# Five half-row runs for two rows, where there were six runs of 384 columns: the first transform stage of an FNet and long-convolution kernel

## The chip, the cores and the metric

The kernel runs on one core of one Trainium2 chip. The metric is the device time of one execution in microseconds. TensorE (PE) multiplies matrices into PSUM banks, VectorE (DVE) and ScalarE (ACT) do arithmetic and move PSUM to SBUF, GpSimd (POOL) and SyncE (SP) issue transfers, and ACT issues transfers as well. Each engine runs its own instructions in the order in which they stand in the program. An instruction that waits holds up all that stand behind it on its engine.

## The reference

The reference is four layers over a matrix of 2048 rows and 576 columns. Two are Fourier mixing layers, two are gated long convolutions:

```python
    x = x + _A_ref(_layernorm(x, axis=-1), A_dft_seq_re, A_dft_seq_im, A_dft_hid_re, A_dft_hid_im)
    x = x + _B_ref(_layernorm(x, axis=-1), B_k, B_v, B_shift_k, B_ssm_k, B_ssm_D)
    x = x + _A_ref(_layernorm(x, axis=-1), A_dft_seq_re, A_dft_seq_im, A_dft_hid_re, A_dft_hid_im)
    x = x + _B_ref(_layernorm(x, axis=-1), B_k, B_v, B_shift_k, B_ssm_k, B_ssm_D)
```

`_A_ref` takes the real part of a two-dimensional discrete Fourier transform, written as products with cosine and sine matrices (2048 by 2048 along the sequence, 576 by 576 along the columns). `_B_ref` computes `q * (y + kv * ssm_D)`, where `kv` is a convolution of `k` with 4 taps, times `v`, and `y` is the convolution of `kv` with `ssm_k` along the sequence, by a Fourier transform of length 4096. `y` doesn't depend on `x`, so it is computed once, beside the first layer.

## The kernel before

The first Fourier layer is the generator `layer`. It goes through steps `(g, tb, k)`: for each of 4 blocks of output rows, for cosine and for sine, for 16 rows `k` of the input. A step multiplies row `k` with a tile of the sequence matrix (128 by 512) in 14 matmuls of 512 columns: for each of four column blocks `dc` three (high by high, high by low, low by high part, since every float is split into two rounded parts), and two for the 64 columns that remain. They go into the PSUM banks `s` (four) and `rm`. The tile of the sequence matrix comes by a DMA (`load_c`) and is split into its parts by `split`: ACT copies the high part (`mats<-flts`), then DVE subtracts (`mats<-flts,mats`). After 16 steps the four banks are evacuated to `u`.

The convolution's transform is the generator `branch`, and its instructions are put between those of the layer. Its first stage has 16 "rows" `j`, each with two sources of 576 columns: `v` (multiplied by the convolved `k`, which DVE computes in `convolve`: 1152 columns an instruction, `f1f<-f1f`) and `ssm_k`. `f1_split(j, src)` makes the parts of a source: for `v` DVE multiplies first (`f1f<-f1f,flts`), then ACT copies the high part (`f1r<-f1f`, for `ssm_k` `f1r<-flts`) and DVE subtracts (`f1r<-f1f,f1r` and `f1r<-flts,f1r`). From the fifth row on (`j >= K_FIRST`) both sources of a row lie side by side in one tile, 1152 columns. The list `todo` sets the order: `(4, v)`, `(4, ssm_k)`, `(5, v)` and so on, and each entry `n` has two half steps, `2n` and `2n + 1`. The list `visits` says from which half step on a run of columns may be multiplied, and one half step takes at most one.

One run is `f1_products`. It takes two of three PSUM banks `bf` by turns (so that every run shares a bank with the run before it), and multiplies the two halves of the partitions apart: 6 matmuls with 64 rows of weights, three parts by two halves, which leave a bank each. ACT then copies both banks to a buffer (`flts<-bf`) and issues the store to `t_d` (`td<-flts`) from its own queue. In the kernel before, a row from the fifth on has three runs of `VW = 384` columns, from the third half step behind its last split, and a store takes both banks at once; the buffers are three of 768 words (`sp`).

The order on every engine comes from a scheduler, which places the recorded instructions by its own estimates of their durations. Each DMA of SP and ACT tells its landing by one of eight counters, `DMAHW0` to `DMAHW7`, given out by turns; a DMA that is given a counter waits until the one that had it before has landed.

In this text the runs of two rows after the change are called A and B (first row), M (the mixed one), C and D (second row), with the row's number behind the letter. Step `n` is the `n`-th step of the layer, counted over all blocks.

Of the kernel before, what the change touches and what calls it, by code (L numbers as in the profile page):

```python
# [12 lines left out]
AF = mybir.ActivationFunctionType  # L13
# [3 lines left out]
HP = P // 2  # L17
S = 2048
D = 576
J = S // P  # L20
TB = 4
NT = 512
HD = D // 2
# [7 lines left out]
ROWS = (0, 1, 2, 3, 4, 5, 6, 7, 8, 9)  # L31
K_FIRST = 4
F1_16 = 5
VW = 384
F1_END = 42
W_FROM = 41
HOLD = 125
# [16 lines left out]
CRAW = 2  # L54
# [6 lines left out]
SC_AT = 8 + 4 * STAT  # L61
# [5 lines left out]
def fnet_h3_kernel(ctx: ExitStack, tc: tile.TileContext, x, c_mat, w_re, w_im, k_pad, v, shift_k,  # L67
                   ssm_k, ssm_d, f1c, i2c, midc, out):
    nc = tc.nc
# [5 lines left out]
    def mm(ps, lhsT, rhs, first, last, more=False):  # L75
        return nc.tensor.matmul(ps, lhsT, rhs, start=first, stop=last, skip_group_check=more).ins  # L76
# [3 lines left out]
    def turn():  # L80
        given[0] += 1
        return banks[(given[0] - 1) % 3]
# [30 lines left out]
    def flat(words, dt, name):  # L113
        return sb.tile([P, words], dt, tag=name, name=name)
# [29 lines left out]
    def two(v):  # L144
        return v.rearrange("p (a n) -> p a n", a=2)
# [11 lines left out]
    flts = flat(FLT, F32, "flts")  # L157
# [5 lines left out]
    anchor, made, rounded, pows, biased, halved, added, evac, parted, stored = [], [], [], [], [], [], [], [], [], []  # L163
# [39 lines left out]
    t_d = dr.tile([P, 2 * J, 2 * D], F32, name="td")  # L203
# [21 lines left out]
    W = {}  # L225

    def load_w():
        lay(flts, SC_AT + CRAW * NT + 4 * D, ("wl", D, 3))
        wg = region_a(FR, "w").rearrange("p (k n) -> p k n", k=9)
        for ch in (8, *range(8)):  # L230
            w = two(wg[:, ch])
            raw = ring["wl"]()
            if ch < 8:
                asked[:] = [nc.sync.dma_start(raw, (w_re if ch < 4 else w_im)[(ch % 4) * P:(ch % 4 + 1) * P, :]).ins]
            else:
                nc.sync.dma_start(raw[:REM], w_re[NC * P:, :])
                nc.sync.dma_start(raw[REM:], w_im[NC * P:, :])
            for lo, hi, sg in ((0, P, 1 if ch < 4 else -1),) if ch < 8 else ((0, REM, 1), (REM, P, -1)):
                if sg > 0:
                    split(w[lo:hi, 0, :], w[lo:hi, 1, :], raw[lo:hi])  # L240
# [15 lines left out]
    U, seq = {}, []  # L256
# [94 lines left out]
    def branch():  # L351
        f1r = region_b(FR, "f1r")
        lay(f1r, 0, ("xf", 2 * D, 4), ("fc", 2 * P, 5))
        lay(f1r, 0, ("xp", 4 * D, 2))
        at = lay(flts, SC_AT + CRAW * NT, ("so", D, 4), ("land", D, 3))
        lay(flts, SC_AT + CRAW * NT, ("sp", 2 * VW, 3))
        lay(flts, at, ("craw", NT, 1))
        f1f = region_a(F32, "f1f")
        ks = f1f[:, :KR * 2 * D]
# [2 lines left out]
        wt, rows, landed, fcs, paired = [], {}, {}, {}, []  # L362
# [23 lines left out]
        def convolve():  # L386
            for i in range(J // 2):
                if not wt:
                    load_w4()
                load_k(i + KR - 1)  # L390
                rp = rows[i] = two(ring["rp"]())
                for t in range(4):
                    out_t = two(tmp) if t else rp
                    for n, k in k_rows(2 * i + t):
                        nc.vector.tensor_tensor(out_t[:, n], k, wt[3 - t][:, n], OP.mult)  # L395
                    yield
                    if t == 1:
                        load_k(i + KR)
                    if t:
                        nc.vector.tensor_tensor(rp, rp, out_t, OP.add)  # L400
                        yield
# [38 lines left out]
            parted[:] = split(h, l, two(r))  # L440
            return tuple(paired)

        def f1_products(j, fc, xf, at, n, so, to):
            ps = [turn()[:, :n] for _ in range(2)]
            last = seq[-1:]
            for k, (a, b) in enumerate(((0, 1), (0, 0), (1, 0))):
                for i in (1, 0):
                    half = slice(i * HP, (i + 1) * HP)
                    with behind(*last):
                        last = [mm(ps[i], fc[half, a, :], xf[b][half, at:at + n], k == 0, k == 2)]  # L450
            so = two(ring[so]())
            for i in range(2):
                stored[:] = [nc.scalar.activation(so[:, i, :], ps[i], AF.Copy).ins]  # L453
            nc.scalar.dma_start(t_d[:, j::J, to:to + n], so)

        conv, made_ops, visits = convolve(), 0, []
# [4 lines left out]
        for n, (j, src) in enumerate(todo):  # L461
            f1_loads(n + 1)
            if n < 2:
                yield
            xf = f1_split(j, src)
            if j < K_FIRST:
                visits += [(2 * n + 2, j, fcs[j], xf, hf * HD, HD, "so", hf * D + src * HD) for hf in range(2)]
            elif src:
                visits += [(2 * n + 3, j, fcs[j], xf, at, VW, "sp", at) for at in range(0, 2 * D, VW)]
            if n:  # L470
                f1_loads(n + 3)
            later = [m for m in range(n + 1, len(todo)) if todo[m][1] == 0 and 7 * (todo[m][0] // 2 + 1) > made_ops]
            for half in range(2):
                visit(2 * n + half)
                if later and n > 2:
                    left = 7 * (todo[later[0]][0] // 2 + 1) - made_ops
                    for _ in range(-(-left // (2 * (later[0] - n) - half)) if left > 0 else 0):
                        next(conv)
                        made_ops += 1
                yield  # L480
# [6 lines left out]
        at = lay(m1, 0, ("df", 2 * D, 3), ("mc", 4 * P, 1))  # L487
# [86 lines left out]
        landed, halves, fcs, yfs = {}, {}, {}, []  # L574
# [193 lines left out]
    wl = load_w()  # L768
# [23 lines left out]
    for n, whole in layer(get_x0, lambda j: x[:, j, :], done0, pending):  # L792
# [3 lines left out]
        if (whole or whole is not None and n % J < J - 1) and n <= F1_END and not part:  # L796
            at = n if whole else n - 0.5
# [234 lines left out]
    for n, whole in layer(get_x1, lambda j: xb_d[j], done1, pending, 1):  # L1032
# [143 lines left out]
```

## Time and profile before

| | before |
|---|---|
| median of 3 runs | 1181.65 us (1181.65 to 1184.18) |
| the profiled execution, its own time | 1182.72 us |
| its span in the profile | 1180.9 us |
| PE busy | 1168.1 us (99%) |
| DVE busy | 868.5 us (74%) |
| ACT busy | 650.9 us (55%) |
| granted TensorE clock | 0.999 |

The rows from the fifth on are multiplied between 92.86 and 196 us of the span, in 36 runs. A busy share is a share of the whole span: an engine with 74% can be without any idle time in one stage.

### The profile page before, as it was taken

To read this page: it belongs to the slowest core of one execution; us is meant where nothing else is said; L and a number is where in the kernel's file an instruction comes from. 1 tells how busy PE (TensorE), PEld (TensorE's weight loads), DVE (VectorE), ACT (ScalarE), POOL (GpSimd) and SP (SyncE) were. 2 spreads that over 40 slices of the span, in tenths; PEclk is the share of its full clock that TensorE was granted. 3 is DMA by queue.
4 is the path that set the end of the run, shared out by engine and by line. 5 is a ranking of instruction groups with operands and counts; after the bars stand their busy time and mean duration, and the time that the engine had idled before them with its cause. 6 is when DMAs were issued, how large, how long until landed. Compare 5 with 4: busy or idle time off the path is not lost.

```text
span 1180.9 us, 18086 instructions
## 1 busy us (share of the span) xinstructions
PE 1168.1 (99%) x6198; PEld 990.1 (84%) x6198; DVE 868.5 (74%) x1564; ACT 650.9 (55%) x1280; POOL 75.5 (6%) x115
## 2 busy tenths in 40 slices
PE   8999999999999999999999999999999999999997
PEld 6776667988888988888888898888888888889997
DVE  7899983788877778777757765965776776775764
ACT  7865655577766667766645666534434445450210
POOL 2310000000000000001101111000000000001111
PEclk9999999999999999999999999999999999999999
DMA  9879898545666656648966776862872787795621
GB/s 330 291 230 310 263 299 279 170 152 170 209 215 200 201 170 192 185 144 246 271 188 221 243 247 228 260 236 76 259 244 72 229 288 247 258 329 160 214 92 41
DMA packets 147453, 255.64 MB, mean 216 GB/s; under 512 B 16161, under 2 KB 56353, under 8 KB 147362
## 3 DMA queue, kind: packets, MB, share of 16 engines
q1 hardware_dynamic: 111890, 210.17, 55.7%
q10 hardware_dynamic: 28560, 37.91, 9.1%
q0 software_dynamic: 6912, 6.43, 2.4%
q8 instruction: 48, 0.79, 0.3%
q14 instruction: 43, 0.35, 0.1%
HBM read 187.80 MB, written 66.65 MB: 215 GB/s over the span
## 4 chain that ended last, share of the span: by engine, by line
PE 86%; DVE 5%; ACT 3%; DMA 3%; issue 2%; SPq 0%; ACTq 0%; POOL 0%; DVEq 0%
PE s L76 49%; PE bk L76 30%; PE rm L76 5%; PE bf L76 2%; DMA flts<-in_c_mat 1%; ACT flts L514 1%; DVE f1f L395 1%; DVE f1f L400 1%; DVE mats L100 1%; ACT mid L514 1%; DVE mid L520 1%; DMA early<-in_x 0%; ACT mats L99 0%; DMA yb<-flts 0%; DMA flts<-td 0%
## 5 line engine op out<-in xcount | busy, mean ns | idle before, releaser
L76 PE MATMUL s<-mats 128*128 128x512 f32 x2102 | 547.0, 396 | 3.9 <-DVE mats L761 1.5
L76 PEld LDWEIGHTS s<-mats 128*128 128x128 f32 x2102 | 383.7, 189 | 85.9 <-issue 11.1
L100 DVE TENSOR_TENSOR mats<-flts,mats 128x512 fp32r<-128x512 f32 x206 | 140.6, 687 | 50.5 <-ACT mats L99 48.9
L99 ACT ACTIVATE mats<-flts 128x512 fp32r<-128x512 f32 x206 | 128.2, 627 | 82.1 <-PE bk L76 31.6
L76 PE MATMUL bk<-mid 128*128 128x288 f32 x704 | 126.6, 301 | 1.5 <-ACT flts L514 0.8
L76 PEld LDWEIGHTS bk<-mid 128*128 128x128 f32 x704 | 108.7, 188 | 21.9 <-ACT flts L514 5.7
L514 ACT ACTIVATE flts<-bk 128x288 f32<-128x288 f32 (+1 forms) x192 | 76.5, 405 | 91.1 <-PE bk L76 76.0
L76 PE MATMUL bk<-w,u 128*128 128x288 f32 x864 | 120.4, 296 | 0.0
L76 PEld LDWEIGHTS bk<-w,u 128*128 128x128 f32 x864 | 117.4, 188 | 2.9 <-ACT flts L514 0.9
L520 DVE TENSOR_TENSOR mid<-flts,mid 128x576 fp32r<-128x576 f32 (+1 forms) x149 | 93.3, 627 | 19.1 <-ACT mid L514 16.3
L76 PE MATMUL rm<-mats 128*128 128x512 f32 x304 | 94.6, 391 | 0.2 <-ACT flts L514 0.2
L514 ACT ACTIVATE mid<-flts 128x576 fp32r<-128x576 f32 (+1 forms) x148 | 80.5, 576 | 9.8 <-DVE flts L535 5.1
L289 DVE TENSOR_TENSOR flts<-flts,bk 128x288 f32<-128x288 f32 x48 | 21.8, 454 | 68.3 <-PE bk L76 68.3
L76 PE MATMUL bk<-mats 128*128 128x288 f32 (+1 forms) x376 | 67.9, 317 | 0.0
L76 PEld LDWEIGHTS rm<-mats 128*128 128x128 f32 x304 | 57.0, 188 | 12.6 <-ACT flts L514 0.6
L453 ACT ACTIVATE flts<-bf 128x384 f32<-128x384 f32 (+1 forms) x104 | 43.2, 462 | 42.6 <-PE bf L76 39.8
L76 PE MATMUL s<-t,mats 128*128 128x512 f32 x264 | 64.9, 389 | 0.0
L186 POOL TENSOR_TENSOR flts<-flts 128x1 f32<-128x1 f32 x34 | 28.0, 823 | 516.4 <-DVE flts L185 514.0
L76 PE MATMUL bk<-mats,t 128*128 128x288 f32 (+1 forms) x368 | 59.3, 303 | 0.0
L514 ACT ACTIVATE flts<-flts 64x288 f32<-64x288 f32 x128 | 56.7, 443 | 4.5
L76 PEld LDWEIGHTS bk<-mats 128*128 128x128 f32 x376 | 55.5, 188 | 3.4
L76 PEld LDWEIGHTS s<-t,mats 128*128 128x128 f32 x264 | 49.6, 188 | 10.3
(152 smaller groups left out, 1495.5 us busy)
## 6 DMA issues: line engine op xcount, KB each, us to landing
flts<-in_c_mat SPq DMA_DIRECT2D x148, 256.0 KB, 3.6
ph<-in_c_mat SPq DMA_DIRECT2D x54, 512.0 KB, 4.1
flts<-in_c_mat SPq DMA_DIRECT2D x30, 512.0 KB, 5.7
flts<-td SPq DMA_DIRECT2D x53, 288.0 KB, 3.0
td<-flts ACTq DMA_DIRECT2D x36, 384.0 KB, 4.4
vd<-flts ACTq DMA_DIRECT2D x64, 144.0 KB, 2.5
flts<-vd SPq DMA_DIRECT2D x32, 288.0 KB, 3.9
ud<-ph ACTq DMA_DIRECT2D x12, 512.0 KB, 6.2
```

The source lines that it names most:

```text
L76: return nc.tensor.matmul(ps, lhsT, rhs, start=first, stop=last, skip_group_check=more).ins
L99: a = nc.scalar.activation(h, src, AF.Copy).ins
L100: return a, nc.vector.tensor_tensor(l, src, h.bitcast(F32), OP.subtract).ins
L186: pows.append(nc.gpsimd.tensor_tensor(rs, ve, mhalf, OP.pow).ins)
L289: added[:] = [nc.vector.tensor_tensor(r[:, cs], r[:, cs], ps[:, :HD], OP.add).ins]
L395: nc.vector.tensor_tensor(out_t[:, n], k, wt[3 - t][:, n], OP.mult)
L400: nc.vector.tensor_tensor(rp, rp, out_t, OP.add)
L453: stored[:] = [nc.scalar.activation(so[:, i, :], ps[i], AF.Copy).ins]
L514: last_act.append(nc.scalar.activation(*args, **kw).ins)
L520: nc.vector.tensor_tensor(l, src, h.bitcast(F32), OP.subtract)
```

## The change

Two rows `j` and `j + 1` (4 and 5, 6 and 7, and so on, six pairs) are multiplied in five runs instead of six. `CUT` gives their widths. A and B take 464 columns each of the first row, M takes the first row's last 224 columns and the second row's first 240, C and D take 456 each. M stands at the third half step behind the split of the second row's `v`; its 240 columns are of `v` alone. It has 12 matmuls, since its two pieces have weights of their own; both pieces lie side by side in the same two banks. A half of a run gets a buffer of its own (five of 464 words) and a store of its own, and M has a store for each piece of each half. So a pair of rows has 36 matmuls before and after, 12 evictions before and 10 after, 6 stores before and 12 after. The first four rows are as before, and the buffers behind (`land`, `wl`) lie 16 words further on.

```diff
-VW = 384
+CUT = (464, 464, 240, 456, 456)
+OUT_END = 5 * CUT[0]
...
-        at = lay(flts, SC_AT + CRAW * NT, ("so", D, 4), ("land", D, 3))
-        lay(flts, SC_AT + CRAW * NT, ("sp", 2 * VW, 3))
+        lay(flts, SC_AT + CRAW * NT, ("so", D, 4))
+        at = lay(flts, SC_AT + CRAW * NT + OUT_END, ("land", D, 3))
+        lay(flts, SC_AT + CRAW * NT, ("sp", CUT[0], 5))
...
-        def f1_products(j, fc, xf, at, n, so, to):
-            ps = [turn()[:, :n] for _ in range(2)]
-            last = seq[-1:]
+        def f1_products(pieces, so):
+            ps, last, at = [turn() for _ in range(2)], seq[-1:], 0
+            placed = []
+            for j, fc, xf, src, n, to in pieces:
+                placed.append((at, fc, xf, src, n))
+                at += n
             for k, (a, b) in enumerate(((0, 1), (0, 0), (1, 0))):
-                for i in (1, 0):
-                    half = slice(i * HP, (i + 1) * HP)
-                    with behind(*last):
-                        last = [mm(ps[i], fc[half, a, :], xf[b][half, at:at + n], k == 0, k == 2)]
-            so = two(ring[so]())
+                for o, fc, xf, src, n in placed:
+                    for i in (1, 0):
+                        half = slice(i * HP, (i + 1) * HP)
+                        with behind(*last):
+                            last = [mm(ps[i][:, o:o + n], fc[half, a, :], xf[b][half, src:src + n],
+                                       k == 0 and o == 0, k == 2, o > 0)]
+            both = two(ring[so]()) if so == "so" else None
             for i in range(2):
-                stored[:] = [nc.scalar.activation(so[:, i, :], ps[i], AF.Copy).ins]
-            nc.scalar.dma_start(t_d[:, j::J, to:to + n], so)
...
+                one = ring[so]() if both is None else both[:, i, :]
+                stored[:] = [nc.scalar.activation(one[:, :at], ps[i][:, :at], AF.Copy).ins]
+                if both is None or i == 1:
+                    for (j, *_, to), (o, *_) in zip(pieces, placed):
+                        for n, cols in to:
+                            if both is None:
+                                nc.scalar.dma_start(t_d[:, j + i * J, cols:cols + n], one[:, o:o + n])
+                            else:
+                                nc.scalar.dma_start(t_d[:, j::J, cols:cols + n], both[:, :, o:o + n])
+                            o += n
...
+            elif not src and j % 2:
+                open_run.append((j, fcs[j], xf, 0, CUT[2], [(CUT[2], 0)]))
+                visits.append((2 * n + 3, list(open_run), "sp"))
+                open_run.clear()
             elif src:
-                visits += [(2 * n + 3, j, fcs[j], xf, at, VW, "sp", at) for at in range(0, 2 * D, VW)]
+                at, widths = (CUT[2], CUT[3:]) if j % 2 else (0, CUT[:2])
+                for i, w in enumerate(widths):
+                    visits.append((2 * n + 2 + j % 2 + i * (2 - j % 2), [(j, fcs[j], xf, at, w, [(w, at)])], "sp"))
+                    at += w
+                if at < 2 * D:
+                    open_run.append((j, fcs[j], xf, at, 2 * D - at, [(2 * D - at, at)]))
```

The scheduler places everything anew in this stage. Three places show it. First DVE from the split of row 5's `ssm_k` on. In the rows `mats` is the sequence tile of a step (the first of them is step 24's), `f1f` the convolution of `k` (with `flts`: the multiplication by row 6's `v`), and `f1r` a split. Before:

```order
L100 TENSOR_TENSOR f1r<-flts,f1r 128x2x288
L400 TENSOR_TENSOR f1f<-f1f 128x1152
L100 TENSOR_TENSOR mats<-flts,mats 128x512
L428 TENSOR_TENSOR f1f<-f1f,flts 128x576
L395 TENSOR_TENSOR f1f<-f1f 128x1152 x2
L100 TENSOR_TENSOR f1r<-f1f,f1r 128x2x288
L100 TENSOR_TENSOR mats<-flts,mats 128x512
```

And now:

```order
L101 TENSOR_TENSOR f1r<-flts,f1r 128x2x288
L402 TENSOR_TENSOR f1f<-f1f 128x1152
L397 TENSOR_TENSOR f1f<-f1f 128x1152
L430 TENSOR_TENSOR f1f<-f1f,flts 128x576
L397 TENSOR_TENSOR f1f<-f1f 128x1152
L101 TENSOR_TENSOR f1r<-flts,f1r 128x2x288
L402 TENSOR_TENSOR f1f<-f1f 128x1152
L101 TENSOR_TENSOR mats<-flts,mats 128x512
L101 TENSOR_TENSOR f1r<-f1f,f1r 128x2x288
```

Step 24's tile stood third and stands eighth now, behind a multiplication and an addition of the convolution and a split; the multiplication of row 6 stands one wide instruction further back. Up to the second row shown the order is the same in both programs.

Second ACT, in the middle of the stage. `bf` with a number is a bank of the runs, and `mats` is as above. The piece begins with the split of row 11's `v`. Before:

```order
L99 ACTIVATE f1r<-f1f 128x2x288
L453 ACTIVATE flts<-bf_66 128x384
L454 DMA td<-flts 256x1x384
L453 ACTIVATE flts<-bf_67 128x384
L453 ACTIVATE flts<-bf_68 128x384
L99 ACTIVATE mats<-flts 128x512
L454 DMA td<-flts 256x1x384
L453 ACTIVATE flts<-bf_67 128x384
L453 ACTIVATE flts<-bf_66 128x384
L99 ACTIVATE mats<-flts 128x512
L99 ACTIVATE f1r<-flts 128x2x288
L99 ACTIVATE f1r<-f1f 128x2x288
```

And now:

```order
L100 ACTIVATE f1r<-f1f 128x2x288
L461 ACTIVATE flts<-bf_67 128x464
L461 ACTIVATE flts<-bf_68 128x464
L100 ACTIVATE mats<-flts 128x512
L466 DMA td<-flts 128x464 x2
L100 ACTIVATE f1r<-f1f 128x2x288
L100 ACTIVATE f1r<-flts 128x2x288
L461 ACTIVATE flts<-bf_67 128x464
L461 ACTIVATE flts<-bf_66 128x464
L100 ACTIVATE mats<-flts 128x512
```

The second `f1r<-f1f` of each piece is the split of row 12's `v`. Five evictions stood between it and row 11's before, two (those of B10) do now, and the evictions of M10 stand behind it; C11 takes `bf_66` next. At row 6 it is the same: its `f1r<-f1f` stands directly ahead of the evictions of C5, one of whose banks D5 takes next.

Third the stores of C7 on ACT, with what each instruction waits for:

```order
L100 ACTIVATE mats<-flts 128x512 [waits DMAHW7_49]
L466 DMA td<-flts 128x456 [waits DMAHW0_49,Activation_49]
L466 DMA td<-flts 128x456 [waits DMAHW1_49]
L461 ACTIVATE flts<-bf_68 128x456 [waits DMAHW4_49,PE_49]
L461 ACTIVATE flts<-bf_66 128x456 [waits DMAHW3_49,DMAHW2_49]
```

Both stores wait for a counter, and behind them stand the evictions of D7, one of whose banks (`bf_68`) A8 takes. Of the stores of these rows, 16 of 36 waited for a counter before, and 46 of 72 do now.

More of the change, by code (lines that the diff above doesn't have):

```diff
@@ L227, in load_w @@
     def load_w():
-        lay(flts, SC_AT + CRAW * NT + 4 * D, ("wl", D, 3))
+        lay(flts, SC_AT + CRAW * NT + OUT_END, ("wl", D, 3))
         wg = region_a(FR, "w").rearrange("p (k n) -> p k n", k=9)
@@ L441, in f1_split @@
             return tuple(paired)
[L443 to L456 removed]
+        def f1_products(pieces, so):
[4 more added lines that the diff above has]
+                at += n
+            for k, (a, b) in enumerate(((0, 1), (0, 0), (1, 0))):
+                for o, fc, xf, src, n in placed:
[5 more added lines that the diff above has]
+            both = two(ring[so]()) if so == "so" else None
+            for i in range(2):
+                one = ring[so]() if both is None else both[:, i, :]
[8 more added lines that the diff above has]
+                            o += n
+        conv, made_ops, visits, open_run = convolve(), 0, [], []
         def visit(half):
@@ L466, in branch @@
             if j < K_FIRST:
-                visits += [(2 * n + 2, j, fcs[j], xf, hf * HD, HD, "so", hf * D + src * HD) for hf in range(2)]
-            elif src:
-                visits += [(2 * n + 3, j, fcs[j], xf, at, VW, "sp", at) for at in range(0, 2 * D, VW)]
+                visits += [(2 * n + 2, [(j, fcs[j], xf, hf * HD, HD, [(HD, hf * D + src * HD)])], "so")
+                           for hf in range(2)]
+            elif not src and j % 2:
+                open_run.append((j, fcs[j], xf, 0, CUT[2], [(CUT[2], 0)]))
+                visits.append((2 * n + 3, list(open_run), "sp"))
+                open_run.clear()
+            elif src:
+                at, widths = (CUT[2], CUT[3:]) if j % 2 else (0, CUT[:2])
[4 more added lines that the diff above has]
+                    open_run.append((j, fcs[j], xf, at, 2 * D - at, [(2 * D - at, at)]))
             if n:
```

## The prediction, made before the changed kernel was run

> **What bounds the kernel now.** I read the page first, then busy time by stretches, then the timelines of the stage that the change touches.
>
> ```profile
> span 1180.9 us, 18086 instructions
> PE 1168.1 (99%) x6198; PEld 990.1 (84%) x6198; DVE 868.5 (74%) x1564; ACT 650.9 (55%) x1280; POOL 75.5 (6%) x115
> ...
> 100.00:150.00 50.00, 49.53 (x250) 34.08 (x248) 47.93 (x56) 29.64 (x60) 2.64 (x5) 1.00 0.89 295
> 150.00:200.00 50.00, 50.00 (x250) 35.09 (x251) 32.27 (x43) 29.86 (x61) 1.05 (x2) 1.00 0.89 278
> ```
>
> PE sets the end: 1168.1 of 1180.9 us. So what PE is spared or made to wait in this stage goes to the end almost one to one. But the third row (PE, PEld, DVE, ACT, POOL, clock, DMA) shows a second engine with nothing to spare: DVE is busy for 47.93 of 50 us between 100 and 150. PE gets its sequence tiles and its splits from DVE in time only because of the order in which DVE does its work, and that order changes.
>
> **The gain: one run fewer in six.** PE's timeline gives the price of a run.
>
> ```profile
> 86.37 0.66 PE L76 MATMUL bf<-f1r 64*128 64x288 f32 x6
> 86.96 3.03 PE L76 MATMUL s<-mats 128*128 128x512 f32 x12
> ...
> 124.55 3.04 PE L76 MATMUL s<-mats 128*128 128x512 f32 x12
> 127.42 0.62 PE L76 MATMUL rm<-mats 128*128 128x512 f32 x2
> 127.97 0.79 PE L76 MATMUL bf<-f1r 64*128 64x384 f32 x6
> 128.69 1.20 PE L76 MATMUL s<-mats 128*128 128x512 f32 x4
> ...
> 198.38 2.88 PE L76 MATMUL s<-mats 128*128 128x512 f32 x12
> 201.10 0.62 PE L76 MATMUL rm<-mats 128*128 128x512 f32 x2
> 201.55 2.88 PE L76 MATMUL s<-mats 128*128 128x512 f32 x12
> ```
>
> A bare step takes 3.17 us (198.38 to 201.55), step 28 with one run 4.14 (124.55 to 128.69): a run of 384 costs 0.97. Its own matmuls are 0.72 of that (127.97 to 128.69); the remaining 0.25 is the way into and out of matmuls of 64 rows: the 12 `s` matmuls behind a run take 2.87 (124.55 to 127.42) instead of 2.72, and the two `rm` ahead of it 0.55 instead of 0.45. A run of 288 takes 0.59 (86.37 to 86.96), so 96 columns are 0.13, and a column 1.35 ns. Then 464 columns cost 0.83 + 0.25 = 1.08, 456 cost 1.07. M has six pairs of short matmuls: 1.08 if only its columns count, 1.28 if the 0.20 us that a run of three pairs spends without columns (0.59 - 288 x 1.35 ns) is paid twice. I take 1.15, nearer to the first, since the 0.25 is what a switch costs. Two rows: 6 x 0.97 = 5.82 before, 2 x 1.08 + 2 x 1.07 + 1.15 = 5.45 after. That is 0.37 us spared (0.24 to 0.44), 2.2 us for six pairs.
>
> The Trainium skill says in "TensorEngine Tiling (Array Packing)", section "Key Properties", that changing the tiling mode drains TensorE; by that rule alone each pair saves one switch, 0.25 us, 1.5 in all, and the trace agrees that there is such a cost. On ACT a pair has two evictions less and six stores more; ACT is busy for 30 of 50 us, so its sum costs nothing. Its order does.
>
> **First loss: DVE's order, to step 28.** The spacing of DVE's instructions and ACT's answer to them:
>
> ```profile
> 98.18 1.34 DVE L395 TENSOR_TENSOR f1f<-f1f 128x1152 f32<-128x1152 f32 x1
> 99.45 0.67 DVE L100 TENSOR_TENSOR mats<-flts,mats 128x512 fp32r<-128x512 f32 x1
> 100.05 0.74 DVE L100 TENSOR_TENSOR f1r<-flts,f1r 128x576 fp32r<-128x576 f32 x1
> 100.72 1.34 DVE L400 TENSOR_TENSOR f1f<-f1f 128x1152 f32<-128x1152 f32 x1
> 101.99 0.67 DVE L100 TENSOR_TENSOR mats<-flts,mats 128x512 fp32r<-128x512 f32 x1
> 102.59 0.74 DVE L428 TENSOR_TENSOR f1f<-f1f,flts 128x576 f32<-128x576 f32 x1
> ...
> 118.56 0.67 DVE L100 TENSOR_TENSOR mats<-flts,mats 128x512 fp32r<-128x512 f32 x1
> ```
>
> ```profile
> 85.57 0.71 ACT L453 ACTIVATE flts<-bf 128x288 f32<-128x288 f32 x2 [2.70 <-PE bf L76]
> ...
> 103.37 0.69 ACT L99 ACTIVATE f1r<-f1f 128x576 fp32r<-128x576 f32 x1 [0.29 <-DVE f1f L428]
> 103.96 0.85 ACT L453 ACTIVATE flts<-bf 128x384 f32<-128x384 f32 x2
> ```
>
> DVE stands without gaps, 1.27 us for a wide instruction, 0.60 for a tile's split, 0.67 for the rest. Up to 101.99 both programs have the same order. Before, 8 wide ones, 6 others and step 28's tile as the fifth tile follow: 10.16 + 4.02 + 4 x 0.60 = 16.58, start at 118.57, and the last DVE row says 118.56. Now 12 wide ones, 10 others and four tiles stand ahead of it: 15.24 + 6.7 + 2.4 = 24.34, start at 126.33, end at 127.0. PE used that tile's low half 0.3 us into step 28, at about 124.85, and would now do so at 127.05: **2.2 us late**.
>
> PE comes there no sooner by the other road. Row 6's multiplication starts one wide instruction from 101.99, at 103.26, and ends at 104.0. ACT splits it (0.6 to the next instruction, as the two ACT rows show) and only then evicts C5: 104.63 plus 1.0 for two (0.71 at 288 columns, 0.85 at 384, so 0.14 for 96), 105.65. There D5 gets its bank: 0.82 for its matmuls, then by the order six `s` (1.51: half of 2.72, and the 0.15 behind a run) and two `rm` (0.45), and step 24 starts at 108.4; four bare steps and five runs (12.68 + 5.45) give 126.55 for step 28. So both roads end within 0.3 us; together I take 2.3 us at step 28 (2.0 to 2.8). The gain of the first two pairs is in this.
>
> **Second loss: stores that wait, steps 28 to 32.**
>
> ```profile
> DMA to landing us min/median/max: 2.8/4.6/6.0
> ...
> td<-flts ACTq DMA_DIRECT2D x36, 384.0 KB, 4.4
> ...
> vd<-flts ACTq DMA_DIRECT2D x64, 144.0 KB, 2.5
> ...
> ACT flts L453 <- DMA td<-flts: 2.6, 1, 2.6
> ```
>
> The first row is the landing of the `ssm_k` loads between 100 and 150 us. C7's second store waits for a counter which the program gave to such a load last, and SP issues that one when DVE has multiplied row 9's `v`, at 123.2 by the placing above. It lands at 126.0 to 129.2; D7's eviction behind it frees A8's bank 0.9 us later; A8 is due at 128.3 (step 28 at 126.85, six `s`, the switch). That is 0 to 1.8, and other stores like it, and half buffers that are used again after two and a half runs instead of three, add 0 to 2: the last row shows one such wait of 2.6 us before. A half store of 237 KB lies between 144 KB (2.5 us) and 384 KB (4.4), so it lands sooner. I take 2.0 (0 to 3.8).
>
> The Trainium skill, "DMA: Bandwidth & Descriptors", section "Rules for kernel authors", says to coalesce small transfers, which speaks against twice as many stores; what it would add here is inside these 3.8 us.
>
> **Third loss: row 12's split ahead of M10's evictions, steps 32 to 36.**
>
> ```profile
> 142.28 0.79 PE L76 MATMUL bf<-f1r 64*128 64x384 f32 x6
> 143.00 3.04 PE L76 MATMUL s<-mats 128*128 128x512 f32 x12
> ...
> 146.33 0.61 PE L76 MATMUL s<-mats 128*128 128x512 f32 x2
> 146.88 0.79 PE L76 MATMUL bf<-f1r 64*128 64x384 f32 x6
> ...
> 144.90 0.69 DVE L100 TENSOR_TENSOR u<-flts,u 64x512 fp32r<-64x512 f32 x1 [0.70 <-ACT u L99]
> ...
> 153.98 0.75 DVE L428 TENSOR_TENSOR f1f<-f1f,flts 128x576 f32<-128x576 f32 x1
> ...
> 154.87 0.68 ACT L99 ACTIVATE f1r<-f1f 128x576 fp32r<-128x576 f32 x1
> 155.44 0.87 ACT L453 ACTIVATE flts<-bf 128x384 f32<-128x384 f32 x2
> ```
>
> I count from the run at 142.28, in whose place A10 stands; a delay so far moves everything. From the evacuation of `u` (144.90) to row 12's multiplication (153.98, end 154.73) DVE's order is the same in both programs, and it hangs on PE's end of step 31. Before, ACT had evicted all runs by then. Now it splits both sources of row 12 first (0.6 each), and M10's two evictions follow at 155.95, end 156.95. PE: A10 0.83, step 32 3.33 (143.00 to 146.33), two `s` 0.55, B10 at 146.99 and 0.83, twelve matmuls 2.97, M10 at 150.8, 0.9, six `s` 1.6: C11 is due at 153.3. It has to wait for `bf_66` until 157.0, **3.7 us** (3 to 4.5).
>
> **The sum.** To step 28 +2.3. Stores +2.0. M10 +3.7. The gain of the other four pairs -1.5. For the last two pairs' own waits of the same kinds I add 0.5 (0 to 2). That makes +7.0 us (+2.5 to +12): 1182.72 + 7.0 = 1189.7 for the profiled execution, which stood 1.07 above the median, so **1188.7**. Behind the stage nothing changes its order, and PE is busy to the end.
>
> **The rivals.** (a) The lateness stays within what PE has in hand, and only the gain is left: 2.2 us less, 1179.5, not slower. For it: PE waited for ACT's evictions once in this stage, for 0.5 us. It decides if tiles come over 2.2 us before their use after the change; step 28's would have to be 7.8 us ahead now, and nothing shows that. Chance 0.08. (b) One of the two large losses doesn't come, because loads that land sooner or later shift ACT's and DVE's order in time: +7.0 - 3.7 or less, +1 to +3.5, 1183 to 1185. Chance 0.14. (c) The waits of stores feed on each other: 46 issues wait for a counter, ACT's queue stands still for each, the loads of SP share the counters, and the sequence tiles come late too. DMA is at 0.89 of its time. Four pairs at 2 us each on top: +10 to +16, 1192 to 1198. Chance 0.16.
>
> **How the numbers follow.** Forecast 0.62, spread over +3.5 to +10. A measurement of this kernel can tell about 0.3%, 3.5 us, from no change. Slower by more: forecast and (c), 0.78. Within: (b) and half of (a), 0.18. Faster by more: half of (a), if the short pairs and switches cost less than the rows say, 0.04. The range leaves out (a) and the upper half of (c): 1183 to 1195.
>
> **What would show it.** In the changed profile: DVE's split of step 28's tile ends near 127.0; PE waits for ACT's evictions (PE and PEld `bf` together) for over 5 us between 90 and 210, the longest about 3.7 around 160, behind M10; ACT waits for DVE's multiplication of row 12 with M10's evictions behind it; a step with one run of 464 takes 4.25. If PE's waits stay under 1 us, DVE's order didn't matter and I am wrong.

## The result: about 8 us slower

| | before | after |
|---|---|---|
| median of six runs | 1181.65 us (1181.34 to 1184.18) | 1190.24 us (1188.94 to 1191.73) |
| ratio | | 1.0068, 95% interval 1.0056 to 1.0081 |
| the profiled execution | 1182.72 us, span 1180.9 | 1191.73 us, span 1189.9 |

The medians lie 8.6 us apart; the ratio of all runs, 1.0068, is 8.0 us. The forecast was 1188.7 us. From the page of the changed kernel, the busy times:

```profile
PE 1167.8 (98%) x6198; PEld 990.3 (83%) x6198; DVE 869.8 (73%) x1564; ACT 649.4 (55%) x1268; POOL 75.5 (6%) x115
```

PE is busy as long as before (1168.1), but the span is 9.0 us longer: PE stands idle for them. The busy times by stretches show the idle time, and a lower clock, in the stage of the change (PE, PEld, DVE, ACT, POOL, clock, DMA):

```profile
100.00:150.00 50.00, 45.81 (x231) 32.28 (x231) 44.08 (x51) 28.59 (x55) 2.63 (x5) 1.00 0.85 276
150.00:200.00 50.00, 45.88 (x230) 32.25 (x228) 33.25 (x42) 25.55 (x48) 0.53 (x1) 0.93 0.78 246
```

PE was busy for 49.53 and 50.00 us in these stretches before. The waits between 90 and 210 us of the changed kernel (sum, number, longest):

```profile
ACT f1r L100 <- DVE f1f L430: 11.1, 6, 5.0
ACT flts L461 <- DMA td<-flts: 9.3, 5, 3.8
PE bf L77 <- ACT flts L461: 8.3, 6, 4.1
```

PE waits for evictions six times, 8.3 us in all, where it was once and 0.5 us. ACT in its turn waits for DVE's multiplications of rows (first row), and with its evictions until stores have landed or have been issued (second row). PE's timeline has the places:

```profile
101.60 0.89 PE L77 MATMUL bf<-f1r 64*128 64x456 f32 x6 [1.39 <-ACT flts L461]
...
105.38 0.89 PE L77 MATMUL bf<-f1r 64*128 64x456 f32 x6 [1.33 <-ACT flts L461]
...
127.15 1.52 PE L77 MATMUL s<-mats 128*128 128x512 f32 x6
...
129.23 0.89 PE L77 MATMUL bf<-f1r 64*128 64x464 f32 x6 [0.56 <-ACT flts L461]
...
160.98 1.51 PE L77 MATMUL bf<-f1r 64*128 64x456 f32 x6 [4.12 <-ACT flts L461]
162.42 2.93 PE L77 MATMUL s<-mats 128*128 128x512 f32 x6
...
184.77 3.02 PE L77 MATMUL s<-mats 128*128 128x512 f32 x12
...
202.75 3.02 PE L77 MATMUL s<-mats 128*128 128x512 f32 x12
...
220.85 0.37 PE L77 MATMUL bk<-mid 128*128 128x288 f32 x1 [0.81 <-DVE flts L290]
```

C5 waits 1.39, D5 1.33, A8 0.56, C11 4.12 us. C11's own matmuls then take 1.51 us where C5's take 0.89, and the six `s` behind it 2.93 instead of 1.6: PE runs at half its clock there. From the row at 184.77 to that at 202.75 go four steps and five runs without a wait; they give the price of a pair further down. ACT's timeline at four places ahead of these waits:

```profile
99.97 0.68 ACT L100 ACTIVATE f1r<-flts 128x576 fp32r<-128x576 f32 x1 [2.31 <-DMA flts<-in_ssm_k]
100.56 0.99 ACT L461 ACTIVATE flts<-bf 128x464 f32<-128x464 f32 x2
...
103.76 0.68 ACT L100 ACTIVATE f1r<-f1f 128x576 fp32r<-128x576 f32 x1 [1.70 <-DVE f1f L430]
...
104.35 0.97 ACT L461 ACTIVATE flts<-bf 128x456 f32<-128x456 f32 x2
...
126.24 2.28 ACTq L466 DMA_DIRECT2D td<-flts  x2
128.63 0.99 ACT L461 ACTIVATE flts<-bf 128x456 f32<-128x456 f32 x2 [3.77 <-DMA td<-flts]
...
158.78 0.68 ACT L100 ACTIVATE f1r<-f1f 128x576 fp32r<-128x576 f32 x1 [4.99 <-DVE f1f L430]
...
159.94 0.99 ACT L461 ACTIVATE flts<-bf 128x464 f32<-128x464 f32 x2
```

At 99.97 the split of row 5's `ssm_k` waits for its load, and M4's evictions stand behind it: that makes C5 late. At 103.76 and at 158.78 a split waits for DVE, for row 6 and row 12, and the evictions of C5 and of M10 stand behind it: that makes D5 and C11 late. At 126.24 two stores keep ACT's queue for 2.28 us, and D7's evictions stand behind them. The brackets at 128.63 name the landing of a store, but the first eviction starts when the second of the two stores has been issued (128.20 and 0.33 us).

### The profile page after: what moved, and what is told of

Same layout as the page of the kernel before. It is cut to its first block, busy times and chain, and to the rows that moved or that the text cites. A ratio compares the mean times of both kernels' runs of the same rounds, so it can differ in the third digit from the quotient of the medians.

```text
span 1189.9 us, 18133 instructions
## 1 busy us (share of the span) xinstructions
PE 1167.8 (98%) x6198; PEld 990.3 (83%) x6198; DVE 869.8 (73%) x1564; ACT 649.4 (55%) x1268; POOL 75.5 (6%) x115
## 4 chain that ended last, share of the span: by engine, by line
PE 75%; ACT 2%; DMA 2%; DVE 2%; issue 1%; ACTq 0%; DVEq 0%
PE s L77 42%; PE bk L77 29%; PE rm L77 4%; ACT flts L540 1%; ACT mid L540 1%; DMA t<-ud 1%; DVE mid L546 0%; DMA yb<-flts 0%; DMA flts<-td 0%; ACT mats L100 0%; DMA flts<-in_c_mat 0%; DVE flts L560 0%; DVE flts L559 0%; DVE flts L558 0%; DVE flts L561 0%
## 5 line engine op out<-in xcount | busy, mean ns | idle before, releaser
L461 ACT ACTIVATE flts<-bf 128x464 f32<-128x464 f32 (+2 forms) x92 | 41.6, 498 | 35.5 <-PE bf L77 26.1
```

The source lines that it names most:

```text
L461: stored[:] = [nc.scalar.activation(one[:, :at], ps[i][:, :at], AF.Copy).ins]
```

## The experiments

The theory: the change takes PE's work away as reckoned, but three things on ACT's queue make evictions late. A split that waits for a full DVE; stores that wait for the landing of another transfer, twice as many as before; and buffers that come free later. The rivals: DVE alone is the limit; half stores alone are; the gain doesn't exist. Ratios are to the kernel before, run beside each of these kernels on the same chip, where its median lay between 1182.55 and 1182.97 us. In all kernels but those of E1 and E11 the scheduler places the stage anew, so more moves than the thing named.

### E1 and E2: one cause at a time

E1 is the changed kernel with row 12's split behind M10's evictions. Nothing else moves on any engine but two stores and two evictions next to it.

```diff
-            parted[:] = split(h, l, two(r))
+            with behind(*(stored if j == 12 and not src else ())): parted[:] = split(h, l, two(r))
```

> The changed kernel, with one instruction moved on ACT: row 12's high-half split, which waits for DVE's multiplication, stands behind the two evictions of the short-pair run M10 instead of ahead of them. Theory (the 4.1 us idle of TensorE at C11 comes from that one place in ACT's order, and the idle itself brings the granted clock down to 0.5 behind it): the wait at C11 is under 0.5 us, the windows 160 to 166 us show clock 1.00, and the time falls by 4.1 of wait and about 2.4 of slow clock, less up to 0.8 for a new wait of D11: 1183.7 to 1184.5 us. Rival A (the low clock has another cause than the idle): the wait goes, the clock stays at 0.5 for some 5 us, about 1186.2. Rival B (DVE is the limit, and another wait takes the place): 1188 or more.

Measured: 1190.87 us (1186.94 to 1192.64), ratio 1.0065 (1.0052 to 1.0079). The profiled execution took 1187.83. On its PE timeline:

```profile
157.07 0.88 PE L77 MATMUL bf<-f1r 64*128 64x456 f32 x6 [0.16 <-ACT flts L461]
...
161.56 0.90 PE L77 MATMUL bf<-f1r 64*128 64x456 f32 x6 [1.57 <-ACT flts L461]
```

On ACT's:

```profile
159.03 0.69 ACT L100 ACTIVATE f1r<-f1f 128x576 fp32r<-128x576 f32 x1 [2.01 <-DVE f1f L430]
159.09 1.82 ACTq L466 DMA_DIRECT2D td<-flts  x2
...
160.95 0.99 ACT L461 ACTIVATE flts<-bf 128x456 f32<-128x456 f32 x2 [0.72 <-issue]
```

C11's wait falls from 4.12 to 0.16 us, so it did come from that one place in the order. But the next run, D11, now waits 1.57 us, twice the 0.8 allowed for: C11's evictions stand behind the moved split and two stores that take 1.82 us to issue. In the profiled execution 3.9 of 9.0 us came back; in the median nothing did, and that is the range of rival B: another wait takes the place. E11 looks at the scatter.

E2 is the kernel before, with half stores only.

```diff
-        lay(flts, SC_AT + CRAW * NT, ("sp", 2 * VW, 3))
+        lay(flts, SC_AT + CRAW * NT, ("sp", VW, 6))
...
+                if both is None:
+                    nc.scalar.dma_start(t_d[:, j + i * J, to:to + n], one)
```

> The kernel before, with its six runs of 384 columns, but each half of a run evicted into its own 384-word buffer (six of them in the same space) and stored by its own transfer: twice the stores, everything else as it was. If half stores make waits of the size that the prediction gave them (2.0 us): 1183.2 to 1184.2 us. If they feed on each other (rival c): 1185 or more. If the second loss was over-sized, as the trace of the changed kernel reads (about 0.5): 1181.3 to 1182.3.

Measured: 1183.86 us (1182.31 to 1185.89), ratio 1.0012 (1.0003 to 1.0020), 0.4 to 2.4 us. By its median that is the first case; against the kernel before on the same chip it is 1.3 us (1183.86 - 1182.55), between the 2.0 us of the prediction's second loss and the 0.5 read from the changed kernel's trace; the interval holds both. ACT's timeline of the profiled execution, the longest of the eleven:

```profile
112.86 2.79 ACTq L456 DMA_DIRECT2D td<-flts  x2
115.76 0.87 ACT L454 ACTIVATE flts<-bf 128x384 f32<-128x384 f32 x2 [3.11 <-DMA flts<-in_c_mat]
```

The second of these two stores starts only at 115.33. It was given the counter of a store that ACT issued at 109.03 and that took 6.3 us to land, and two evictions stand behind it. The brackets name a load, which these evictions didn't need. The run that needs their bank waited 1.67 us. So half stores make such waits in a kernel with the old runs too, with six half buffers.

### E3 and E4: where C11's wait comes from, and a shorter one

E3 takes the wide runs only from row 8 on; rows 4 to 7 have runs of 384 at the old places, stored by halves, from the changed kernel's five half buffers.

```diff
+WIDE_ROWS = range(8, 16)
...
+            elif j not in WIDE_ROWS:
+                if src:
+                    visits += [(2 * n + 3, [(j, fcs[j], xf, c, 384, [(384, c)])], "sp") for c in range(0, 2 * D, 384)]
             elif not src and j % 2:
```

> The changed kernel, but rows 4 to 7 (the two pairs in the stretch where DVE is saturated) in runs of 384 at the old places, stored by halves; the five wide runs only from row 8 on. Theory 1 (the loss at C11 is made locally, by M10's place against row 12's split): the first loss goes with the gain of two pairs, the wait at C11 and the low clock stay: 1187 to 1188 us. Theory 2 (C11's wait is inherited from the lateness and the DVE order of the first two pairs): both losses go, four pairs gain 0.37 each: 1179.8 to 1181.0.

Measured: 1190.80 us (1189.87 to 1191.15), ratio 1.0069 (1.0057 to 1.0081): above both. PE's timeline:

```profile
113.48 0.79 PE L78 MATMUL bf<-f1r 64*128 64x384 f32 x6 [2.68 <-ACT flts L462]
...
160.39 1.51 PE L78 MATMUL bf<-f1r 64*128 64x456 f32 x6 [3.84 <-ACT flts L462]
```

C11 waits as it did, so its wait is made on the spot and not handed on from the first pairs (theory 2 falls). And rows 4 to 7 wait as long with half stores and the old runs, 2.68 us at one place, as C5 and D5 do in the changed kernel together (1.39 + 1.33). That wait has another cause, as ACT's timeline shows:

```profile
110.29 0.47 ACT L462 ACTIVATE flts<-bf 128x384 f32<-128x384 f32 x1
112.94 0.49 ACT L462 ACTIVATE flts<-bf 128x384 f32<-128x384 f32 x1 [2.18 <-DMA td<-flts]
```

No store stands between the two evictions. The second waits for its buffer: the store that last used it, five stores back, was issued at 104.76 and took 8.1 us to land. So it is the number of buffers that makes PE wait here, and not ACT's queue.

E4 leaves out one addition of DVE ahead of row 12's multiplication.

```diff
-                        nc.vector.tensor_tensor(rp, rp, out_t, OP.add)
+                        if i != 6 or t < 3: nc.vector.tensor_tensor(rp, rp, out_t, OP.add)
```

> The changed kernel, leaving out one addition of 128x1152 on DVE (the last of the four-tap sum for rows 12 and 13; rows 12 and 13 of the filter lack one tap), which stands 1.35 us long ahead of the multiplication that row 12's split waits for. Both theories: the idle at C11 falls from 4.1 to about 2.8 us. Theory (the clock falls only behind an idle longer than some length between 1.4 and 4.1 us, and 2.8 is below it): clock 1.00 throughout, 1186 to 1187 us. Rival (the clock falls here too): 0.5 behind the idle again, 1188.5 to 1189.2.

Measured: 1190.56 us (1188.49 to 1191.57), ratio 1.0065 (1.0052 to 1.0078). C11 waited 3.0 us, 1.1 less, and the clock fell to 0.5 behind it all the same, for 3.4 us instead of 6.8. The rival is right on the clock. The time lies above both ranges; C9 had a new wait of 1.07 us, for evictions behind a split that waited for a load of `ssm_k`.

### E5, E6, E7, E9: DVE and the queue, each and both

Two kernels leave out two of four taps of the convolution on DVE, E5 from the kernel before, E6 from the changed one.

```diff
-                    for n, k in k_rows(2 * i + t):
+                    for n, k in k_rows(2 * i + t) if t < 2 else ():
...
-                        nc.vector.tensor_tensor(rp, rp, out_t, OP.add)
+                        if t < 2: nc.vector.tensor_tensor(rp, rp, out_t, OP.add)
```

> The kernel before, leaving out the taps t = 2 and 3 of the four-tap sum on DVE (two multiplications and two additions of 128x1152 for each pair of rows, about 5 of 9 us of DVE work a pair; the filter has two taps). DVE is no longer full between 84 and 139 us. All theories: TensorE is the bound as before, its only wait in the stage (0.47 us) may go: 1181 to 1182.5 us. It is the partner of the next run.

> The changed kernel with the same taps left out. Theory 1 (the losses come from a full DVE, which hands row 6's and row 12's multiplications and the tiles' splits over late): the waits for evictions go, the clock stays at 1.00 and only the gain is left, 2.2 us under the light kernel before: 1179 to 1180.5. Theory 2 (the half stores in ACT's queue make waits of their own, whatever DVE does): 1 to 2 us over it, 1182 to 1184. If ACT's order alone makes them: 1185 or more.

E7 is the changed kernel with the stores of the wide runs issued by POOL, E9 has this and the taps left out.

```diff
-                                nc.scalar.dma_start(t_d[:, j + i * J, cols:cols + n], one[:, o:o + n])
+                                nc.gpsimd.dma_start(t_d[:, j + i * J, cols:cols + n], one[:, o:o + n])
```

> The changed kernel, with the half stores of the wide runs issued by POOL instead of ACT, so that no eviction stands behind a store that waits. The scheduler then also puts row 12's split behind M10's evictions by itself, and step 28's tile ahead by some instructions on DVE. Theory (stores in ACT's queue and ACT's order make the second and third loss): waits of TensorE between 120 and 165 us under 1 us in sum, clock 1.00, first loss and gain left: 1182 to 1184. Rival (the evictions are late whoever stores, since their inputs or DVE are): 1187 or more.

> The changed kernel with both suspects taken away at once: the taps t = 2 and 3 left out of DVE's sum (as in the two light kernels) and the half stores issued by POOL. Theory (nothing but ACT's held-up queue and the full DVE costs the change its gain): waits of TensorE for evictions between 90 and 205 us under 1 us in sum, and 1.5 to 2.2 us less than the light kernel before with its 1181.3: 1179.1 to 1180. Rival (the gain of 0.37 us a pair does not exist, or the runs' new places cost it): 1181 to 1182.5.

| | DVE as it is | taps left out |
|---|---|---|
| runs of 384, stores by ACT | 1 | E5: 1181.30 us, 0.9989 (0.9980 to 0.9998) |
| wide runs, stores by ACT | 1.0068 (1.0056 to 1.0081) | E6: 1186.56 us, 1.0034 (1.0021 to 1.0046) |
| wide runs, stores by POOL | E7: 1185.82 us, 1.0024 (1.0015 to 1.0033) | E9: 1182.09 us, 0.9990 (0.9981 to 1.0000) |

Each column is read downwards. E5 is where it was expected. With DVE full the change costs 8 us, with a light DVE 5.3 (1186.56 - 1181.30). So a full DVE is a part of it, not the whole: theory 1 of E6 falls, and the 1 to 2 us of theory 2 are too few. E6's waits (from 90 to 205 us) name the rest:

```profile
ACT flts L461 <- DMA flts<-in_v: 4.7, 1, 4.7
...
ACT flts L461 <- DMA f1f<-in_k_pad: 4.0, 1, 4.0
```

Evictions are held up for 4.7 and 4.0 us by the landings of loads of `v` (and of `ssm_k` before it) and of `k`. An eviction needs none of them; a store ahead of it on ACT's queue does, since it was given the counter of that load. PE waits 1.79 us at D5 and 1.85 at A12 for it, while DVE stands idle.

With the stores off ACT the cost falls to 2.9 us with a full DVE (above the 1182 to 1184 expected). With a light one it is 0.8 by the medians and 0.1 by the ratios, so it is within the noise. E7 has another order too: row 12's split stands behind M10's evictions, as in E1. E1 has that move alone and was no faster, so most of the 5 us must come with the stores; step 28's tile, which also moved on DVE, was not tested by itself. E7's clock stays at 1.00, and its waits are:

```profile
ACT flts L461 <- DMA td<-flts: 16.6, 7, 4.3
...
PE bf L77 <- ACT flts L461: 3.8, 6, 1.4
```

Evictions still wait for stores to land, without a store ahead of them in ACT's queue: that is the buffers. PE's waits are C5 and D5 above all (0.92 us behind the split of row 5's `ssm_k`, 1.40 where row 6's split still waits for DVE). Between 120 and 165 us PE waits 2.5 us in all, 1.3 of them for evictions, where under 1 was expected. E9 was expected under 1180 us and isn't. One wait over 0.3 us is left:

```profile
156.61 0.99 ACT L461 ACTIVATE flts<-bf 128x456 f32<-128x456 f32 x2 [4.04 <-DMA td<-flts]
```

ACT does nothing for 4 us there: the eviction waits until the store that last used its buffer has landed. PE's run behind it waits 1.64 us.

### E12: the buffers

E12 is E9 with seven half buffers instead of five. The two more lie where the weights of the taps that are left out were, and these weights are no longer loaded.

```diff
         lay(f1f, KR * 2 * D, ("wt", 2 * D, 2), ("rp", 2 * D, 2))
+        lay(f1f, KR * 2 * D, ("sp", CUT[0], 2))
```

> The light kernel with stores on POOL, and two more half buffers (seven instead of five), laid over the weights of the two taps that the light kernels leave out, whose load is left out too. What is left of the change's cost in the kernel with five buffers is one wait of 1.6 us in which an eviction waits for its buffer's store to land, and 0.5 us of smaller ones. Theory (five half buffers, which are two and a half runs where there were three, are the last of the causes): no wait for evictions over 0.3 us between 90 and 205 us, and 1.3 to 2.2 us under the light kernel before (1181.3): 1179.1 to 1180.0. Rival (the waits have another cause, or others take their place): 1181.5 to 1182.5 as with five buffers.

Measured: 1180.26 us (1178.19 to 1183.33), ratio 0.9979 (0.9970 to 0.9988), 1.0 us under E5. The time lies between the two ranges. PE has one wait for evictions left between 90 and 205 us, 0.97 us near the stage's end; the one at 157 us is gone. No wait over 0.3 us was expected, and the intervals of E5 and E12 overlap. So with a DVE that has time, stores off ACT's queue and buffers enough, no loss is left; that the change is then a gain, of about half of what was expected, is likely but not clear of the noise.

### E8: the other queue

E8 is E7 with SP in place of POOL (`nc.sync.dma_start`).

> As the run before it, but the half stores are issued by SP, where the loads of the sequence tiles and rows queue too. Theory: as on POOL, 1182 to 1184, as long as no load that is needed soon stands behind a store on SP that waits for its eviction. Rival (the stores only move their waits to SP, and the loads of tiles and rows come late, so DVE and TensorE wait for those): 1186 or more, with waits of ACT or DVE for loads of 2 us and more between 100 and 165 us.

Measured: 1190.11 us (1187.85 to 1190.77), ratio 1.0063 (1.0049 to 1.0077). That is the rival's range, and a wait has the size that it named. ACT's timeline:

```profile
101.37 0.68 ACT L100 ACTIVATE f1r<-flts 128x576 fp32r<-128x576 f32 x1 [3.75 <-DMA flts<-in_ssm_k]
```

A split waits 3.75 us for a load of `ssm_k`, PE 2.03 us at the run behind it. In the changed kernel the same split waits 2.31 us. SP issued the load 0.4 us later here (96.44 instead of 96.07), and it took 4.8 us to land instead of 3.8. SP itself waits 20.2 us for evictions with its stores, 18 times between 90 and 205 us, and its loads stand behind them. That this, and not the slower landing, makes the time is not shown.

### E10: wide runs for the last two pairs only

E10 leaves rows 4 to 11 as in the kernel before, whole stores included, and makes the five wide runs for rows 12 to 15 only, stored by POOL as in E7. The buffers of both kinds lie in the same place.

```diff
+WIDE_FROM = 12
...
+        lay(flts, SC_AT + CRAW * NT, ("so3", 768, 3))
...
-            both = two(ring[so]()) if so == "so" else None
+            both = two(ring[so]()) if so != "sp" else None
...
+            elif j < WIDE_FROM:
+                if src:
+                    visits += [(2 * n + 3, [(j, fcs[j], xf, c, 384, [(384, c)])], "so3") for c in range(0, 2 * D, 384)]
```

> Rows 4 to 11 exactly as in the kernel before (runs of 384, whole stores from ACT), the five wide runs only for rows 12 to 15, where DVE is no longer full, their half stores issued by POOL. Theory: no waits, two pairs gain 0.37 each, 0.7 us under the kernel before: a ratio of 0.9994 (0.9988 to 1.0), and steps 44 to 47 are 0.7 us earlier than in the trace of before. Rival (each switch to the new layout costs a wait of its own): 1.0 to 1.5 us slower.

Measured: 1181.10 us (1180.05 to 1183.93) beside 1182.78, ratio 0.9990 (0.9982 to 0.9999). On PE's timeline step 35 and step 46 start at:

```profile
155.44 1.08 PE L78 MATMUL s<-mats 128*128 128x512 f32 x4
...
202.83 2.88 PE L78 MATMUL s<-mats 128*128 128x512 f32 x12
```

47.39 us lie between them. In the kernel before these steps start at:

```profile
156.48 1.08 PE L76 MATMUL s<-mats 128*128 128x512 f32 x4
...
204.73 2.88 PE L76 MATMUL s<-mats 128*128 128x512 f32 x12
```

They are 48.25 us apart. That is 0.86 us for two pairs, without any wait in either stretch. In its profile E10 is 1.0 us ahead at step 35 already, before the first wide run, which is not the change's. The interval, 0.1 to 2.1 us, holds the 0.86 and only just leaves out zero.

### E11: why E1's runs differ

> The kernel with row 12's split moved, once more, for a second profile: its six runs lay between 1186.9 and 1192.6 us, and the one profiled was among the short ones. Theory: the waits for evictions are not of fixed length (a store in ACT's queue waits for a load to land, and the windows in which the clock is granted lie elsewhere in each execution), so the wait at D11 and the number of slow-clock windows of 3.4 us differ from the first profile's 1.57 us and one window. Rival: the same waits, and the scatter comes from elsewhere.

Measured: 1190.83 us. The same program, but D11 now waits 0.91 us instead of 1.57, and the longest wait is D13's, 2.48 us, which had 0.28 in the first profile. Two windows of 3.4 us have half the clock in this stage, where it was one. On PE's timeline:

```profile
181.76 1.51 PE L77 MATMUL bf<-f1r 64*128 64x456 f32 x6 [2.48 <-ACT flts L461]
```

On ACT's:

```profile
179.42 1.19 ACTq L466 DMA_DIRECT2D td<-flts  x2
180.71 0.99 ACT L461 ACTIVATE flts<-bf 128x456 f32<-128x456 f32 x2 [1.70 <-DMA flts<-in_w_im]
```

Here the stores stood behind a load of `w_im`. How long a store waits hangs on when some load lands, and this is another moment in the two executions. That the long runs of E1 are all of this kind was seen in one of them only.

## Why the prediction came near, and where it was off

**The gain was too small in it.** Two rows were put at 5.45 us. Between 184.77 and 202.75 lie four steps and the five runs of rows 14 and 15: 17.98 - 4 x 3.17 = 5.30. The step with one run of 464 takes 4.23 (184.77 to 189.00; 4.25 was expected), M costs 1.22 (1.15), C and D 0.99 each (1.07). So a pair gains 0.52 in the changed kernel and 0.43 in E10, not 0.37, and six pairs 2.6 to 3.1 us, not 2.2. An estimate from E12, 1.0 us under E5 with a wait of 1.0 us left, is about 2.0 in all.

**The first loss** was right to 0.3 us. Step 28 starts at 127.15, 2.6 us later than before (2.3 was expected). On DVE's timeline

```profile
126.15 0.69 DVE L101 TENSOR_TENSOR mats<-flts,mats 128x512 fp32r<-128x512 f32 x1
```

its tile's split ends at 126.84; 127.0 was worked out from the order. PE itself came by the other road, and never waited for this tile: D5, behind row 6's split, starts at 105.38, where 105.65 was worked out. Two things in the 2.6 us were not seen. C5's 1.39 us come from the load of row 5's `ssm_k`; they cost nothing of their own, since C5's evictions had to wait for row 6's split in any case. And C7's 0.40 and D7's 0.52 us fall ahead of step 28 too. M6's evictions stand behind row 8's split, which waits for DVE (119.16), and C7's behind M6's four stores, which take 1.93 us on ACT's queue without any wait for a counter. Fewer buffers or waiting stores bring as much lateness at the same rows: E3 loses 2.68 us there with the old runs, and E6 1.79 us with a DVE that has time.

**The second loss** was too large in it: 2.0 us behind step 28, where A8's 0.56 are all that PE waits. The mechanism is the one that was named, down to the load. C7's second store starts at 128.20. SP issued the `ssm_k` load that had its counter at 123.06 (123.2 was worked out), and it landed 5.1 us later; D7's evictions behind the store start after 3.77 us in which ACT does nothing. A8's wait lies in the 0 to 1.8 us worked out for it; the other stores and the buffers, put at up to 2, made PE wait for nothing more there. E2 measures half stores by themselves at 1.3 us (0.4 to 2.4). Such waits aren't bound to steps 28 to 32: E2, E6 and E11 have them at three other places.

**The third loss** had the place, the cause and the length: 3.7 us expected at C11, 4.12 measured, gone when one split is moved (E1). What was missing stands behind it. The clock fell to 0.5 for 6.8 us, and PE, busy for 4.8 of them, lost half of that, 2.4 us.

**The sum** came out near since the misses cancel, and that is luck. In its terms: 2.6 to step 28 (2.3 was expected), 0.6 for stores (2.0), 4.1 for M10 (3.7), -1.7 to -2.1 for the gain of the other four pairs (-1.5), nothing for the last two pairs' waits (0.5); and what it put at nothing, 2.4 for the slow clock and 0.8 for the wait at 220.85. That is 8.4 to 8.8 of the 9.0 us of span, where 7.0 were forecast. "Behind the stage nothing changes" was wrong by the wait of 0.8 us, which the kernel before doesn't have. ACT waits 4.70 us for a load of `w_im` there, until 213.16, and its splits of tiles and then DVE are late behind it; why that load comes late stays open.

**The rivals.** (a), that the lateness stays within what PE has in hand, is wrong at six places. (b), that one large loss fails to come, is in none of the six runs (1188.94 to 1191.73). (c), that waiting stores feed on each other, did not come in full; but in E2 a store did wait for a store, and the stores are a larger part of the loss than PE's waits for them alone say: E7 takes them off ACT's queue, and 8 us become 2.9.

## What to carry to other kernels

A store on the queue of an engine that also evicts is not free because the engine has idle time: here it waited for the landing of whatever it shared a counter with, and every eviction behind it waited too. So count the stores that may wait, not the bytes. And before runs are made wider to save switches, find out whether the engines that feed them have time: the same change is a gain of 0.4 to 0.5 us a pair where no eviction is late (E10, and rows 14 and 15 of the changed kernel), and a loss of 8 us where they are.

## What the chip did that was not expected

The clock. All stretches of the granted clock in these records end on a grid of 3.41 us, and the grid lies elsewhere in each execution. Each row below is one such window (PE busy is the first pair of numbers, the clock the third number from the end). The changed kernel:

```profile
155.55:158.96 3.41, 1.31 (x6) 0.74 (x4) 3.41 (x5) 0.18 (x1) 0.43 (x1) 1.00 0.76 231
158.96:162.37 3.41, 1.39 (x6) 0.83 (x6) 3.41 (x5) 2.48 (x5) 0.00 (x0) 0.50 0.75 201
162.37:165.79 3.42, 3.42 (x10) 2.48 (x8) 3.42 (x5) 0.99 (x2) 0.00 (x0) 0.50 0.79 204
```

E1:

```profile
159.17:162.59 3.42, 1.85 (x11) 1.05 (x10) 3.42 (x5) 2.06 (x4) 0.00 (x0) 1.00 0.88 257
162.59:166.00 3.41, 3.41 (x9) 2.64 (x9) 3.41 (x5) 1.76 (x4) 0.00 (x0) 0.50 0.91 251
```

E3, at its wait of 2.68 us:

```profile
108.80:112.21 3.41, 2.01 (x12) 1.14 (x8) 3.41 (x5) 1.07 (x3) 0.00 (x0) 1.00 0.98 351
112.21:115.63 3.42, 2.15 (x12) 1.68 (x13) 2.24 (x3) 1.69 (x4) 0.00 (x0) 1.00 0.97 329
115.63:119.04 3.41, 3.41 (x19) 2.39 (x18) 3.41 (x4) 2.26 (x5) 0.53 (x1) 1.00 0.79 270
```

E11:

```profile
99.81:103.22 3.41, 1.75 (x11) 0.99 (x10) 3.41 (x4) 2.10 (x4) 0.00 (x0) 1.00 0.87 265
```

And the end of E10, where PE finishes with matmuls of 128 rows:

```profile
1171.65:1175.06 3.41, 1.75 (x14) 1.52 (x12) 1.51 (x4) 0.29 (x1) 0.00 (x0) 1.00 0.00 0
1175.06:1178.47 3.41, 0.00 (x0) 0.00 (x0) 1.45 (x4) 0.00 (x0) 0.00 (x0) 1.00 0.25 87
```

These rows read as if what a window held decided on the next. In E1 PE was idle for 1.57 us of one (3.42 - 1.85), and the next had half the clock. In E3 2.68 us of waiting fell into two windows, 1.40 and 1.27 us in each, and the clock stayed. In the changed kernel the slow window itself had 2.0 us of idle time, and the one behind it was slow as well; that one was full, and the clock came back at 165.79. So a wait of 1.6 us may cost another 1.7 (half of a full window), or nothing, as the grid happens to lie; one of 4.1 us cost 2.4. This can be a second source of scatter between executions of one program: E1 and E11 have one and two slow windows. Idle time is not the whole of the rule: E10's window had 1.66 us of it and kept the clock, E11's had as much, and the next window had half the clock. E11's held a run with 64 rows of weights, E10's none; whether that counts was not tested. Such a run isn't needed: the changed kernel's window with 2.1 us of idle time (155.55 to 158.96) held six `s` alone and lost the clock.

The Trainium skill, "TensorE: Matmul & The Clock Gate", Part 1, has the same window, 3413 ns and free-running, and the trace agrees. It lets the clock fall after an idle window; here 1.57 idle microseconds of 3.42 were enough in E1, and 1.40 were not in E3.
